# A linear-attention and two-MoE kernel: the scans' constant moves to another PSUM bank, and the small loads, the gate's bias and the padding rows move to other engines and times

## The chip, the cores and the metric

The kernel runs on one core of one Trainium2 chip. The metric is the time of one execution in microseconds, the median of three runs. Five engines work side by side, each on its own queue in order: TensorE (PE), VectorE (DVE), ScalarE (ACT), GpSimd (POOL) and SyncE (SP), which only issues DMAs here.

## The reference

```python
def _attn_ref(q, k, v, alpha):                 # 4 batches, 8 heads, 768 steps, 48 wide
    for t in range(S):
        state = alpha[:, :, t, :, None] * state + einsum('bhd,bhe->bhde', k[:, :, t], v[:, :, t])
        y[:, :, t] = einsum('bhd,bhde->bhe', q[:, :, t], state)
...
def _moe_ref(x, modality_id, w_gate, modality_bias, w1, w2):     # 3072 tokens, 8 experts
    logits = x @ w_gate + modality_bias[modality_id]
    e_idx = np.argmax(logits, axis=1)
...
        out[mask] = gate_w[mask, None] * (np.maximum(x[mask] @ w1[e], 0.0) @ w2[e])
...
def _moe2_ref(x, w_in, w_out):
    r = np.maximum(x @ w_in, 0.0)
    return (r * r) @ w_out
```

## The kernel before

The work has three parts. The attention goes over 24 chunks of 128 steps (4 batches of 6), and the gate of the first MoE goes along with it; then come the first MoE, sorted by expert, and the second MoE. Only the first part is touched. The order on each engine is that in which the program is written.

A chunk's q, k and alpha lie in one tile `qk` of 112 rows: two heads of 48 rows each, with 16 padding rows between them. `load` fetches it in two pieces for chunks 0 to 2 and in one piece from chunk 3 on. `prep(n)` is the DVE's part of a chunk: a scan forward (`acum`), a reciprocal, a scan backward (`rs`), and two products `qt` and `kt`. Between the two scans stands `kv_sd`, which reads what TensorE put into the PSUM tile `kvc`. Each scan has a second operand `amin`, one constant per row, repeated along the row; it lies in a column of `kvc`. The tracking of waits goes by tiles, so a scan that reads `amin` waits for TensorE's last write into `kvc`, and a write into `kvc` waits for the last scan, though they touch other columns.

TensorE's part of a chunk: `qk_mm` (into the two `sp` tiles, which ACT copies out as `pm`), `k_T` (transposes, which ACT copies out as `kT`), `kv_mm` (from `kT` into `kvc`) and `y_mm` (from `pm`, after GpSimd's `mask` has cleared the upper triangle of it). Iteration n of the loop does `qk_mm(n+1)`, `k_T(n+1)`, `kv_mm(n)`, `mask(n+1)`, `prep(n+3)`, `y_mm(n)`. After every fourth chunk `gate_lg` multiplies the outputs by the gate's weights into the PSUM tile `gps`, ACT copies them, and `back` transposes them into another part of `gps`; `gate_b` writes ranks there too. Ahead of the loop TensorE runs 8 matmuls on a constant tile (`warm(WARM)`) and 5 more (`warm(FILL)`) between `k_T(0)` and `qk_mm(1)`.

DMAs have eight counters, DMAHW0 to DMAHW7, which SP's and ACT's DMAs share. The first eight DMAs take them in turn: chunk 0 takes 0 and 1, chunk 1 takes 2 and 3, the first `vv` takes 4, chunk 2 takes 5 and 6, chunk 3 takes 7. A DMA that gets a counter again is issued only when the DMA that had it has landed, and the engine that issues it waits that long, with all that stands behind it in its queue.

`setup_bias` builds the gate's bias from the modality of each token; `setup_gate` builds constants and ends with a DMA that clears `pbuf`.

Of the kernel before, what the change touches and what calls it, by code (L numbers as in the profile page):

```python
# [11 lines left out]
F32 = mybir.dt.float32  # L12
# [3 lines left out]
I32 = mybir.dt.int32  # L16
# [11 lines left out]
C = 128  # L28
# [29 lines left out]
def body(ctx, tc, qka, v, alpha, mod, wg, mbias, w1, w2, w_in, w_out, out):  # L58
# [44 lines left out]

    def load(n):
        b, c = divmod(n, NCH)
        qk = ld.tile([RP, 2 * NP * C + NP * CA], F32, tag="qk", name="qk", bufs=4)
        if n < 3:
            SY.dma_start(qk[:, 2 * NP * C:], qka[b, c, :, 2 * NP * C:])
            SY.dma_start(qk[:, :2 * NP * C], qka[b, c, :, :2 * NP * C])
        else:  # L110
            SY.dma_start(qk, qka[b, c])
        return qk

    loaded, vs = {}, {}
# [9 lines left out]
    make_identity(nc, ident)  # L124
    A.copy(const.tile([128, 1], F32, name="act0"), ident[:, :1])
    kvc = ps_a.tile([RP, 512], F32, name="kvc")
    amin = kvc[:, 2 * NP * D:2 * NP * D + 1]
    V.memset(amin, AMIN)
    amin = amin.to_broadcast([RP, NP * CA])
    sdt = [at1.tile([RP, SDW], F32, name=f"sd{i}") for i in range(3)]  # L130
# [11 lines left out]
    wg_sb = gc.tile([RP, NP, 32], F32, name="wg_sb")  # L142
    G.memset(wg_sb, 0.0)
    for j in range(2):
        SY.dma_start(wg_sb[64 * j:64 * j + D, :, :NE], wg.rearrange("(p j d) e -> j d p e", j=2, d=D)[j])
    mod_sb = gc.tile([128, NTILE, 2], I32, name="mod_sb")
    SY.dma_start(mod_sb, mod.bitcast(I32).rearrange("p (t w) -> p t w", w=2))
    mb_sb = gc.tile([128, 2, NE], F32, name="mb_sb")
    SY.dma_start(mb_sb, mbias.rearrange("(o m) e -> o m e", o=1).to_broadcast([128, 2, NE]))

    ones_b = gc.tile([128, 128], BF16, name="ones_b")
    lt_b = gc.tile([128, 128], BF16, name="lt_b")
    iot = {}
# [28 lines left out]
    def setup_gate():  # L182
        G.memset(ones_b, 1.0)
        G.affine_select(out=lt_b, in_=ones_b, pattern=[[1, 128]], compare_op=ALU.is_gt, fill=0.0, base=0, channel_multiplier=-1)
        iota_f("rev", [128, 128], [[-1, 128]], 127, 0, F16)
        iota_f("tokid", [128, NTILE], [[128, NTILE]], -NT // 2, 1)
        iota_f("hidx", [128, HC], [[1, HC]], 0, 0)
        iota_f("slj", [128, NBIG + 1], [[1, NBIG + 1]], 0, 0)
        iota_f("edesc", [128, NE], [[-1, NE]], NE, 0)
        iota_f("eidx", [128, NE], [[1, NE]], 0, 0)  # L190
        G.memset(ones8, 1.0)
        G.memset(run, 0.0)
        G.memset(oh_all, 0.0)
        SY.dma_start(pbuf.rearrange("(o n) -> o n", n=C), sdt[2][:(NT + PAD) // C, :C].bitcast(I32))

    def setup_bias():
        modf = gc.tile([128, NTILE, 1], F32, name="modf")
        V.tensor_copy(modf, mod_sb[:, :, 0:1])
        modn = gc.tile([128, NTILE, 1], F32, name="modn")
        V.tensor_scalar(modn, modf, -1.0, 1.0, op0=ALU.mult, op1=ALU.add)  # L200
        lb1 = gc.tile([128, NTILE, NE], F32, name="lb1")
        shp = [128, NTILE, NE]
        V.tensor_tensor(lbias, mb_sb[:, 0:1, :].to_broadcast(shp), modn.to_broadcast(shp), op=ALU.mult)
        V.tensor_tensor(lb1, mb_sb[:, 1:2, :].to_broadcast(shp), modf.to_broadcast(shp), op=ALU.mult)
        V.tensor_add(lbias, lbias, lb1)

    def over(t, sh):
        return t.rearrange("p (o e) -> p o e", o=1).to_broadcast(sh)

    gst = {}  # L210

    def gate_lg(g, i0, i1):
        t0 = GROUPS[g][0]
        lt = gps[:, :128]
        for p in range(NP):
            for i in range(i0, i1):
                q = slice(32 * (i - i0), 32 * (i - i0 + 1))
# [327 lines left out]

    def y_mm(n):
        vv, pm, pr = vs.pop(n), pms.pop(n), preps[n]
        y = ps_a.tile([128, 2, 512], F32, tag="y", name="y")
        cross = n % NCH > 0
        v2 = vv.rearrange("s h d -> s (h d)")  # L550
        quads = [(p, j, HEAD[p][j] % 2, p // 2, (64, D)[HEAD[p][j] % 2]) for p in range(NP) for j in range(2)]
# [199 lines left out]
    preps[0] = prep(0)  # L751
    setup_gate()
    qk_mm(0)
    mask(0)
    k_T(0)
    warm(FILL)
    preps[1] = prep(1)
    loaded[4] = load(4)
    preps[2] = prep(2)
    todo = {}  # L760

    def at(n, where, f):
        todo.setdefault((n, where), []).append(f)
# [557 lines left out]
```

## Time and profile before

| | us |
|---|---|
| median of 3 runs (lowest to highest) | 776.43 (776.18 to 777.32) |
| the profiled execution | 774.81 |
| its span, first to last instruction | 773.0 |
| TensorE busy in the span | 745.1 |
| VectorE busy | 478.0 |
| ScalarE busy | 323.8 |
| GpSimd busy | 166.2 |

The attention part fills about the first 122 us of the span. Time is told from the span's start. A matmul in float32 shows as two records in the trace, and engines overlap one instruction's end with the next one's start by about 0.1 us.

### The profile page before, as it was taken

Reading aid. Unit: us, or ns where it says so; the run is one execution under the profiler, and the core shown is the slowest. Engines: PE = TensorE matmul, PEld = TensorE weight load, DVE = VectorE, ACT = ScalarE, POOL = GpSimd, SP = SyncE. Lnnn points to the kernel's source line nnn. Section 1 sums busy time; section 2 is a strip of 40 time slices with the busy share of each in tenths; the row PEclk is TensorE's granted clock in tenths of the full one; section 3 lists DMA queues with packets and bytes.
Section 4 is the critical chain, followed back from the end, with each engine's and each line's share of the span. In section 5 each row is a group of like instructions: output and inputs, shape, how many; then the busy total and the mean of one; then the engine's idle time right before and its main releaser. Section 6 shows DMA issues by size and latency. Waiting matters only on the chain.

```text
span 773.0 us, 13143 instructions
## 1 busy us (share of the span) xinstructions
PE 745.1 (96%) x5148; PEld 654.0 (85%) x5148; DVE 478.0 (62%) x812; ACT 323.8 (42%) x587; POOL 166.2 (21%) x185
## 2 busy tenths in 40 slices
PE   8898989999999999999999999999999999999994
PEld 6777778898788888889889989999899998999984
DVE  7999997877887867878744444544553333343340
ACT  3446467354444443546533323332332342333340
POOL 3332323234645454431100100010020001002001
PEclk9999999999999999999999999999999999999998
DMA  8988765579877886788300220040010000001001
GB/s 216 266 210 237 208 212 164 167 199 221 158 278 221 214 221 157 251 159 230 126 5 1 66 85 0 11 140 1 0 42 2 1 10 31 1 1 42 0 1 45
DMA packets 42814, 88.89 MB, mean 115 GB/s; under 512 B 11181, under 2 KB 26567, under 8 KB 42743
## 3 DMA queue, kind: packets, MB, share of 16 engines
q1 hardware_dynamic: 39543, 78.13, 36.1%
q0 software_dynamic: 3200, 9.83, 4.6%
q8 instruction: 42, 0.69, 0.4%
q14 instruction: 29, 0.24, 0.1%
HBM read 72.19 MB, written 15.76 MB: 114 GB/s over the span
## 4 chain that ended last, share of the span: by engine, by line
PE 76%; DVE 5%; DMA 2%; ACT 1%; issue 1%; POOL 0%; POOLq 0%; DVEq 0%; ACTq 0%
PE acc L660 8%; PE acc L658 8%; PE acc L659 8%; PE h L659 8%; PE h L660 8%; PE h L658 8%; PE hps L659 4%; PE hps L660 4%; PE oo L658 4%; PE oo L659 4%; PE oo L660 4%; PE hps L658 4%; DMA xg<-xs,ids 1%; DVE w2l L569 1%; PE xt L651 1%
## 5 line engine op out<-in xcount | busy, mean ns | idle before, releaser
L1044 DVE TENSOR_TENSOR r<-r 128x512 f32<-128x512 f32 x96 | 68.7, 716 | 143.8 <-ACT r L1043 143.7
L660 PE MATMUL acc<-w2h,hl 128*128 128x384 f32 x372 | 125.7, 338 | 0.3 <-DVE hl L569 0.2
L658 PE MATMUL acc<-w2h,hh 128*128 128x384 f32 x372 | 125.3, 337 | 0.6 <-ACT hh L568 0.6
L659 PE MATMUL acc<-w2l,hh 128*128 128x384 f32 x372 | 124.9, 336 | 0.0
L1043 ACT ACTIVATE r<-h 128x512 f32<-128x512 f32 x96 | 57.4, 598 | 154.4 <-PE h L660 153.0
L660 PE MATMUL h<-xh,w1l 128*128 128x512 f32 x288 | 113.8, 395 | 0.0
L659 PE MATMUL h<-xl,w1h 128*128 128x512 f32 x288 | 113.6, 395 | 0.0
L658 PE MATMUL h<-xh,w1h 128*128 128x512 f32 x288 | 112.1, 389 | 0.0
L569 DVE TENSOR_TENSOR hl<-r,hh 128x512 fp32r<-128x512 f32 x93 | 64.5, 694 | 63.9 <-PE acc L660 36.4
L1067 POOL DMA_INDIRECT out_dram<-ob,pidx x24 | 23.9, 995 | 366.4 <-ACT ob L1065 328.8
L568 ACT CAST hh<-r 128x512 fp32r<-128x512 f32 x93 | 57.7, 620 | 80.6 <-DVE r L1044 80.6
L658 PEld LDWEIGHTS acc<-w2h,hh 128*128 128x128 f32 x372 | 69.9, 188 | 5.1 <-ACT hh L568 1.0
L659 PEld LDWEIGHTS acc<-w2l,hh 128*128 128x128 f32 x372 | 69.8, 188 | 3.8
L660 PEld LDWEIGHTS acc<-w2h,hl 128*128 128x128 f32 x372 | 69.8, 188 | 1.0 <-DVE hl L569 1.0
L658 PE MATMUL oo<-hh,w2h 128*128 128x512 f32 (+1 forms) x192 | 68.7, 358 | 0.0
L658 PE MATMUL hps<-xh,w1h 128*128 128x512 f32 (+1 forms) x192 | 68.1, 355 | 0.0
L659 PE MATMUL hps<-xl,w1h 128*128 128x512 f32 (+1 forms) x192 | 67.4, 351 | 0.7 <-DVE xl L569 0.7
L660 PE MATMUL oo<-hh,w2l 128*128 128x512 f32 (+1 forms) x192 | 67.3, 350 | 0.0
L659 PE MATMUL oo<-hl,w2h 128*128 128x512 f32 (+1 forms) x192 | 67.2, 350 | 0.0
L660 PE MATMUL hps<-xh,w1l 128*128 128x512 f32 (+1 forms) x192 | 67.1, 350 | 0.0
L660 PEld LDWEIGHTS h<-xh,w1l 128*128 128x128 f32 x288 | 54.0, 188 | 11.5
L659 PEld LDWEIGHTS h<-xl,w1h 128*128 128x128 f32 x288 | 54.0, 187 | 9.2
(217 smaller groups left out, 1281.0 us busy)
## 6 DMA issues: line engine op xcount, KB each, us to landing
qk<-qka_dram SPq DMA_DIRECT2D x21, 679.0 KB, 5.7
raw<-w_dram SPq DMA_DIRECT2D x21, 512.0 KB, 8.1
raw<-w_dram SPq DMA_DIRECT2D x28, 384.0 KB, 4.2
cvr<-w_in_dram SPq DMA_DIRECT2D x12, 512.0 KB, 5.9
cvr<-w_out_dram SPq DMA_DIRECT2D x12, 512.0 KB, 11.6
vv<-v_dram SPq DMA_DIRECT2D x24, 192.0 KB, 6.7
xs<-xb SPq DMA_DIRECT2D x24, 192.0 KB, 3.5
alr<-alpha_dram SPq DMA_DIRECT2D x9, 512.0 KB, 3.4
```

The lines of the kernel that those rows point to most:

```text
L568: A.copy(hi, raw)
L569: V.tensor_sub(lo, raw, hi)
L651: PE.transpose(xt[:, hf * 128:(hf + 1) * 128], xgs[i][:, hf, k * 128:(k + 1) * 128], ident)
L658: PE.matmul(o, ah, bh, start=start, stop=False)
L659: PE.matmul(o, ah, bl, start=False, stop=False)
L660: PE.matmul(o, al, bh, start=False, stop=stop)
L1043: A.activation(r, o, AF.Relu)
L1044: V.tensor_mul(r, r, r)
L1067: G.indirect_dma_start(out=out, out_offset=bass.IndirectOffsetOnAxis(ap=pidx[:, n:n + 1], axis=0), in_=ob, in_offset=None)
```

## The change

The constant `amin` moves from `kvc` to the last column of `gps`, and the gate's logits of the groups inside the loop go into free columns of the output tile `y` of the chunk before, not into `gps`. The loads of the gate's weights, of the modalities and of the bias table and the clearing of `pbuf` are issued by ACT. The five instructions of `setup_bias` run on GpSimd, ahead of the loop. `mask(0)` stands behind `prep(1)` and waits for its last DVE instruction. The `qk` tiles are four fixed ones; from chunk 4 on a load writes only the two times 48 rows with data, in two DMAs.

```diff
@@ load
-        qk = ld.tile([RP, 2 * NP * C + NP * CA], F32, tag="qk", name="qk", bufs=4)
+        if n < 4:
+            qks.append(ld.tile([RP, 2 * NP * C + NP * CA], F32, name=f"qk{n}", bufs=1))
+        qk = qks[n % 4]
...
+        elif n == 3:
+            SY.dma_start(qk, qka[b, c])
         else:
-            SY.dma_start(qk, qka[b, c])
+            for j in range(2):
+                SY.dma_start(qk[64 * j:64 * j + D], qka[b, c, 64 * j:64 * j + D])
...
-    amin = kvc[:, 2 * NP * D:2 * NP * D + 1]
+    gps = ps_g.tile([128, 512], F32, name="gps")
+    amin = gps[:RP, 511:512]
...
-        SY.dma_start(wg_sb[64 * j:64 * j + D, :, :NE], wg.rearrange("(p j d) e -> j d p e", j=2, d=D)[j])
+        A.dma_start(wg_sb[64 * j:64 * j + D, :, :NE], wg.rearrange("(p j d) e -> j d p e", j=2, d=D)[j])
...
-    SY.dma_start(mod_sb, mod.bitcast(I32).rearrange("p (t w) -> p t w", w=2))
+    A.dma_start(mod_sb, mod.bitcast(I32).rearrange("p (t w) -> p t w", w=2))
...
-    SY.dma_start(mb_sb, mbias.rearrange("(o m) e -> o m e", o=1).to_broadcast([128, 2, NE]))
+    A.dma_start(mb_sb, mbias.rearrange("(o m) e -> o m e", o=1).to_broadcast([128, 2, NE]))
@@ setup_gate
-        SY.dma_start(pbuf.rearrange("(o n) -> o n", n=C), sdt[2][:(NT + PAD) // C, :C].bitcast(I32))
+        A.dma_start(pbuf.rearrange("(o n) -> o n", n=C), sdt[2][:(NT + PAD) // C, :C].bitcast(I32))
@@ setup_bias (the four others likewise)
-        V.tensor_copy(modf, mod_sb[:, :, 0:1])
+        G.tensor_copy(modf, mod_sb[:, :, 0:1])
@@ gate_lg, y_mm
-        lt = gps[:, :128]
+        lt = gps[:, :128] if n_y[0] is None else n_y[0][:, 0, 2 * C:3 * C]
...
-        y = ps_a.tile([128, 2, 512], F32, tag="y", name="y")
+        y = n_y[0] = ps_a.tile([128, 2, 512], F32, tag="y", name="y")
@@ ahead of the loop
     qk_mm(0)
-    mask(0)
     k_T(0)
     warm(FILL)
     preps[1] = prep(1)
+    mask(0, last_dve())
+    setup_bias()
     loaded[4] = load(4)
...
-    at(2, "mid", setup_bias)
```

ACT's queue at the program's start, before: the casts of the gate's constants (`rev` to `eidx`), then the copies that `qk_mm(0)` and `k_T(0)` wait to be taken out by.

```order
L125 COPY act_121<-ident 128x1 [waits Pool_49]
L160 CAST rev<-rev_i 128x128 [waits Pool_49]
L160 CAST tokid<-tokid_i 128x24 [waits Pool_49]
L160 CAST hidx<-hidx_i 128x22 [waits Pool_49]
L160 CAST slj<-slj_i 128x6 [waits Pool_49]
L160 CAST edesc<-edesc_i 128x8 [waits Pool_49]
L160 CAST eidx<-eidx_i 128x8 [waits Pool_49]
L507 COPY pm<-sp 128x512 [waits PE_49] x2
```

The same place in the changed kernel:

```order
L151 DMA wg_sb<-wg_dram 48x4x8 [waits DMAHW0_49,Pool_49]
L151 DMA wg_sb<-wg_dram 48x4x8 [waits DMAHW1_49]
L153 DMA mod_sb<-mod_dram 128x48 [waits DMAHW2_49]
L155 DMA mb_sb<-mbias_dram 128x16 [waits DMAHW4_49]
L165 CAST rev<-rev_i 128x128 [waits Pool_49]
L165 CAST tokid<-tokid_i 128x24 [waits Pool_49]
L165 CAST hidx<-hidx_i 128x22 [waits Pool_49]
L165 CAST slj<-slj_i 128x6 [waits Pool_49]
L165 CAST edesc<-edesc_i 128x8 [waits Pool_49]
L165 CAST eidx<-eidx_i 128x8 [waits Pool_49]
L199 DMA pbuf<-sd_128 26x128 [waits DMAHW7_49]
L513 COPY pm<-sp 128x512 [waits PE_49] x2
```

Five DMAs with their counters now stand ahead of ACT's first copy of `pm`; the last of them has the counter of chunk 3's load.

SP's queue behind its first eight loads, before: two `vv` loads, the small loads, the clearing of `pbuf`, then the loads of chunks 4 and 5.

```order
L101 DMA vv<-v_dram 128x384 [waits DMAHW0_49]
L101 DMA vv<-v_dram 128x384 [waits DMAHW1_49]
L145 DMA wg_sb<-wg_dram 48x4x8 [waits DMAHW2_49,Pool_49]
L145 DMA wg_sb<-wg_dram 48x4x8 [waits DMAHW3_49]
L147 DMA mod_sb<-mod_dram 128x48 [waits DMAHW4_49]
L149 DMA mb_sb<-mbias_dram 128x16 [waits DMAHW5_49]
L194 DMA pbuf<-sd_127 26x128 [waits DMAHW6_49]
L111 DMA qk<-qka_dram 112x1552 [waits DMAHW7_49,DVE_49]
L111 DMA qk<-qka_dram 112x1552 [waits DMAHW0_49,DVE_49]
```

The same place in the changed kernel (`qk_99` is the tile of chunks 0, 4, 8 and so on, `qk_102` that of chunks 1, 5, 9):

```order
L101 DMA vv<-v_dram 128x384 [waits DMAHW3_49]
L101 DMA vv<-v_dram 128x384 [waits DMAHW5_49]
L116 DMA qk_99<-qka_dram 48x1552 [waits DMAHW1_49,DMAHW6_49,DMAHW0_49,DVE_49]
L116 DMA qk_99<-qka_dram 48x1552 [waits DMAHW0_49]
L116 DMA qk_102<-qka_dram 48x1552 [waits DMAHW2_49,DMAHW1_49,DVE_49]
L116 DMA qk_102<-qka_dram 48x1552 [waits DMAHW2_49]
```

The small loads are gone from there, each load of a chunk is two DMAs, and the load of chunk 4 waits for the counters 0, 1 and 6, no longer for 7.

DVE's queue from the product `kt` of chunk 5 to the forward scan of chunk 6, before (`SCALAR_TENSOR_TENSOR` is a scan here):

```order
L483 TENSOR_TENSOR kt<-qk,rs 112x512 [waits DVE_49]
L198 CAST modf<-mod_sb 128x24 [waits DMAHW4_49]
L200 TENSOR_SCALAR modn<-modf 128x24 [waits DVE_49]
L203 TENSOR_TENSOR lbias<-mb_sb,modn 128x192 [waits DMAHW5_49,DVE_49]
L204 TENSOR_TENSOR lb_433<-mb_sb,modf 128x192
L205 TENSOR_TENSOR lbias<-lbias,lb_433 128x192 [waits DVE_49]
L472 SCALAR_TENSOR_TENSOR acum<-qk,kvc 112x528 [waits DMAHW2_49,PE_49]
```

And in the changed kernel, up to the first read of `kvc` in chunk 6:

```order
L489 TENSOR_TENSOR kt<-qk_102,rs 112x512 [waits DVE_49]
L478 SCALAR_TENSOR_TENSOR acum<-qk_107,gps 112x528 [waits DMAHW5_49,DMAHW4_49]
L479 RECIPROCAL qk_107<-acum 112x4 [waits DVE_49]
L549 TENSOR_TENSOR sd_126<-kvc,sd_128 112x192 [waits PE_49,Pool_49]
L483 SCALAR_TENSOR_TENSOR rs<-qk_107,gps 112x528 [waits DVE_49]
```

The five instructions of the bias have left DVE, and the forward scan has no wait for TensorE there; that wait now stands at the instruction that reads `kvc`. Of the 24 forward scans 18 waited for a matmul into `kvc` before; 7 wait for one into `gps` now: those of chunks 7, 11, 15 and 19 for `back`, 12 and 20 for `gate_b`, and 23 for the matmuls of the first slot's ids, which stand behind `back`.

## Rows read from the trace of the kernel before

**Rows 1.** The page, part 1: busy us (share of span) and instructions of each engine.

```profile
PE 745.1 (96%) x5148; PEld 654.0 (85%) x5148; DVE 478.0 (62%) x812; ACT 323.8 (42%) x587; POOL 166.2 (21%) x185
```

**Rows 2.** Busy time by stretch: us, each engine's busy us, clock, DMA share, GB/s.

```profile
100.00:120.00 20.00, 18.79 (x332) 15.57 (x332) 17.42 (x42) 12.99 (x30) 8.10 (x13) 1.00 0.67 225
```

**Rows 3.** The chain that ended last, 60 to 126 us: start, us, what.

```profile
105.90 0.60 PE xtr L293 x4
```

**Rows 4.** Waits, 0 to 130 us: who waited for whom, us in total, times, longest.

```profile
PE kvc L529 <- DVE rs L477: 4.9, 7, 1.1
DVE acum L472 <- DMA qk<-qka_dram: 3.6, 2, 2.7
DVE acum L472 <- PE kvc L529: 2.4, 4, 1.1
```

**Rows 5.** Timeline of DVE: start, us, line, instruction, [idle before <- what ended it].

```profile
10.23 1.07 DVE L481 TENSOR_TENSOR qt<-qk,acum 112x512 f32<-112x512 f32 x1
...
14.92 0.67 DVE L481 TENSOR_TENSOR qt<-qk,acum 112x512 f32<-112x512 f32 x1
...
16.11 1.25 DVE L472 TENSOR_TENSOR_SCAN acum<-qk,kvc 112x528 f32<-112x528 f32 x1
...
17.48 0.33 DVE L541 TENSOR_TENSOR sd<-kvc,acum 112x192 f32<-112x192 f32 x1
...
21.00 1.25 DVE L472 TENSOR_TENSOR_SCAN acum<-qk,kvc 112x528 f32<-112x528 f32 x1 [0.84 <-DMA qk<-qka_dram]
...
28.95 0.17 DVE L198 CAST modf<-mod_sb 128x24 f32<-128x24 int32 x1
...
30.30 1.24 DVE L472 TENSOR_TENSOR_SCAN acum<-qk,kvc 112x528 f32<-112x528 f32 x1
...
50.43 1.25 DVE L472 TENSOR_TENSOR_SCAN acum<-qk,kvc 112x528 f32<-112x528 f32 x1 [0.33 <-PE kvc L529]
...
80.22 1.25 DVE L472 TENSOR_TENSOR_SCAN acum<-qk,kvc 112x528 f32<-112x528 f32 x1 [0.58 <-PE kvc L529]
```

**Rows 6.** Timeline of TensorE, the first two chunks, and two places later.

```profile
9.80 2.34 PE L136 MATMUL warm<-wrm 112*128 112x256 f32 x10
12.48 1.16 PE L504 MATMUL sp<-qt,kt 48*128 48x128 f32 x16 [0.34 <-DVE kt L483]
...
15.06 0.61 PE L529 MATMUL kvc<-vv,kT 128*64 128x48 f32 x15 [0.88 <-DVE rs L477]
...
50.31 0.33 PE L226 MATMUL gps<-ident,ls 128*128 128x128 f32 x1
...
97.72 0.61 PE L293 MATMUL xtr<-ident,yt 112*128 112x112 f32 x4 [1.62 <-ACT xb L297]
```

**Rows 7.** Timeline of ACT: the first copies of `pm`.

```profile
9.46 1.07 ACT L507 COPY pm<-sp 128x512 f32<-128x512 f32 x2 [5.49 <-PE sp L504]
```

**Rows 8.** Timeline of SP's DMA issues: start, us the issuing took, line.

```profile
12.77 0.41 SPq L194 DMA_DIRECT2D pbuf<-sd  x1
15.68 1.73 SPq L111 DMA_DIRECT2D qk<-qka_dram  x2
```

**Rows 9.** DMA packets in the stretch 14 to 16 us.

```profile
DMA packets 877, 0.29 MB, mean 144 GB/s; under 512 B 711, under 2 KB 874, under 8 KB 877
```

**Rows 10.** Timeline of GpSimd: its product of 192 columns.

```profile
22.79 0.52 POOL L544 TENSOR_TENSOR sd<-sd,acum 112x192 f32<-112x192 f32 x1 [1.29 <-DVE sd L543]
```

**Rows 11.** Busy time by stretch at the span's end; the clock stands behind GpSimd's column.

```profile
763.00:763.50 0.50, 0.25 (x2) 0.00 (x0) 0.00 (x0) 0.21 (x1) 0.00 (x0) 1.00 0.04 15
...
765.00:765.50 0.50, 0.00 (x0) 0.00 (x0) 0.00 (x0) 0.00 (x0) 0.50 (x1) 0.91 0.00 0
765.50:766.00 0.50, 0.00 (x0) 0.00 (x0) 0.00 (x0) 0.00 (x0) 0.23 (x1) 0.50 0.00 0
```

**Rows 12.** The tile `warm`: ns shortest/median/longest, starts; 1 to 5 us, then 9 to 13.

```profile
L136 PE MATMUL warm<-wrm x8: 634/634/796, 1.7 to 4.8; 112*128 112x256 f32 x8
...
L136 PE MATMUL warm<-wrm x10: 379/379/395, 9.8 to 11.8; 112*128 112x256 f32 x10
```

More of the change, by code (lines that the diff above doesn't have):

```diff
@@ L109, in load @@
             SY.dma_start(qk[:, :2 * NP * C], qka[b, c, :, :2 * NP * C])
-        else:
-            SY.dma_start(qk, qka[b, c])
+        elif n == 3:
+            SY.dma_start(qk, qka[b, c])
+        else:
+            for j in range(2):
+                SY.dma_start(qk[64 * j:64 * j + D], qka[b, c, 64 * j:64 * j + D])
         return qk
-    loaded, vs = {}, {}
+    loaded, vs, qks = {}, {}, []
     for n in range(2):
@@ L153, in body @@
     iot = {}
-    gps = ps_g.tile([128, 512], F32, name="gps")
     def iota_f(name, shape, pattern, base, cm, dt=F32):
@@ L193, in setup_gate @@
         G.memset(oh_all, 0.0)
-        SY.dma_start(pbuf.rearrange("(o n) -> o n", n=C), sdt[2][:(NT + PAD) // C, :C].bitcast(I32))
+        A.dma_start(pbuf.rearrange("(o n) -> o n", n=C), sdt[2][:(NT + PAD) // C, :C].bitcast(I32))
     def setup_bias():
         modf = gc.tile([128, NTILE, 1], F32, name="modf")
-        V.tensor_copy(modf, mod_sb[:, :, 0:1])
+        G.tensor_copy(modf, mod_sb[:, :, 0:1])
         modn = gc.tile([128, NTILE, 1], F32, name="modn")
-        V.tensor_scalar(modn, modf, -1.0, 1.0, op0=ALU.mult, op1=ALU.add)
+        G.tensor_scalar(modn, modf, -1.0, 1.0, op0=ALU.mult, op1=ALU.add)
         lb1 = gc.tile([128, NTILE, NE], F32, name="lb1")
         shp = [128, NTILE, NE]
-        V.tensor_tensor(lbias, mb_sb[:, 0:1, :].to_broadcast(shp), modn.to_broadcast(shp), op=ALU.mult)
-        V.tensor_tensor(lb1, mb_sb[:, 1:2, :].to_broadcast(shp), modf.to_broadcast(shp), op=ALU.mult)
-        V.tensor_add(lbias, lbias, lb1)
+        G.tensor_tensor(lbias, mb_sb[:, 0:1, :].to_broadcast(shp), modn.to_broadcast(shp), op=ALU.mult)
+        G.tensor_tensor(lb1, mb_sb[:, 1:2, :].to_broadcast(shp), modf.to_broadcast(shp), op=ALU.mult)
+        G.tensor_add(lbias, lbias, lb1)
     def over(t, sh):
@@ L210, in body @@
     gst = {}
+    n_y = [None]
     def gate_lg(g, i0, i1):
         t0 = GROUPS[g][0]
-        lt = gps[:, :128]
+        lt = gps[:, :128] if n_y[0] is None else n_y[0][:, 0, 2 * C:3 * C]
         for p in range(NP):
@@ L849, in body @@
     actx.close()
+    n_y[0] = None
     ps_y = pool(gctx, "ps_y", space=PSUM, side="right")
```

## The prediction

> **What bounds the kernel now.** I read the page first. TensorE is busy 96% of the span [rows 1], so what follows the attention is a row of matmuls, and a microsecond won or lost ahead of it is won or lost at the end. The change touches only the attention, the first 122 us. There the view by stretches shows two engines near full side by side, TensorE with 18.8 of 20 us and DVE with 17.4 [rows 2], and nothing throttled. The chain that ended last runs through that part from 105.9 us on, and it is TensorE's queue [rows 3]; before that, records are missing and the chain can't be followed, so I lay out the two queues myself from the timeline.
>
> The waits say how the two hold each other. TensorE's `kv_mm` waited 4.9 us in 7 places for a backward scan; DVE's forward scans waited 2.4 us in 4 places for `kv_mm`, and 3.6 us in 2 places for a load [rows 4], of which 0.84 us lies at chunk 4 [rows 5] and the rest is the first load, which nothing here changes.
>
> **The change, part by part.** The profiled execution took 774.81 us, 1.8 more than its span; the median is 776.43. I work out a difference and put it on the median.
>
> *The bias.* It takes DVE from 28.95 to 30.30 us, where the next scan follows at once [rows 5]: 1.35 us off a full queue. On GpSimd it is three products of 192 columns and two small instructions; a product of that width took 0.52 us there [rows 10], so about 2 us, behind `mask(0)` and ahead of `mask(1)`. GpSimd sits idle in that stretch, and `y_mm(1)`, which needs `mask(1)`, comes late anyway (below). Were the products twice as slow, `mask(1)` and what follows would be up to 1 us later. I count no cost, and 1 us for the upper end.
>
> *The loads.* A load of 96 rows for 112 saves a seventh of the bytes. DVE waited for no load but the two named, so the bytes are worth nothing by themselves. What counts is chunk 4: its load was issued at 15.68 us, because the clearing of `pbuf` stood ahead of it until 12.77 and then it waited for counter 7 [rows 8]. Now it waits for counters 0, 1 and 6, and counter 6 is the one for which `pbuf` waited until 12.77. It goes out nearly 3 us earlier, and the 0.84 us at 21.00 go. That the load is two DMAs is one more issue of some 0.4 us on SP, which has time.
>
> *`mask(0)`.* It ran beside `qt` of chunk 1, which took 1.07 us there and 0.67 in chunk 2 [rows 5]. Moving it gives DVE 0.4 us and perhaps as much on the product behind it. But chunk 3's load lands only at about 15.7 (below) and the scan that needs it began at 16.11, so at most 0.4 of that can be used, and the next step hides all of it.
>
> *The small loads on ACT.* This is the cost. ACT's queue now holds five DMAs ahead of its first copy of `pm`, and the last waits for counter 7, which is chunk 3's load. When does that land? SP's issue at 15.68 was waiting for the same counter; its other wait, `prep(0)`, had long been met. So ACT is held until 15.68, spends 0.41 us on the issue as SP did [rows 8], and makes the two copies in 1.07 us [rows 7]: they end at 17.16, where they ended at 10.53. `qk_mm(1)` needs both `sp` tiles back; it began at 12.48 and begins at 17.16 now. From its start to the end of `kv_mm(0)` lay 15.67 - 12.48 = 3.19 us, of which 0.88 was a wait for a scan [rows 6] that the change removes: 2.31 us of work, so 19.47. DVE's read of `kvc` stood at 17.48 [rows 5] and now waits for that: 2.0 us later.
>
> *TensorE's clock.* `warm(FILL)` ends at 12.14 [rows 6], so TensorE now stands idle for 5.0 us. At the span's end its last matmul is over at about 763.25, and in the stretch from 765.0 the granted clock falls from full to half, 2.2 us later [rows 11]. An idle time of 1.62 us in the middle [rows 6] left it full. [...] Then the 2.31 us become up to 4.62: `kv_mm(0)` ends at 21.78, and DVE is 4.3 us late. If the clock stays up, 2.0 late; with the ratio 634 to 379 in place of two, 3.5.
>
> *The scans' constant.* It takes away false waits, but some come back. Seven forward scans now wait for a matmul into `gps`, among them three of the four that waited in the profile. At 50.43 the scan waited for `kvc`; now it would wait for the transposition behind it, from 50.31 to 50.64 [rows 5, 6]. The same stands at chunks 15 and 23. Only the 0.58 us at 80.22 [rows 5] are surely gone. TensorE's 4.9 us are waits in a queue that was early; they let it catch up, which it needs now, but where the gate's choices come from DVE it still follows DVE. I count 0.3, between 0 and the 2.4 of all four.
>
> *The sum.* Late by 4.3, less 0.84, 1.35 and 0.3: 1.8 us slower, 778.2 us. TensorE begins 4.7 us late and loses 2.3 more at the low clock; the waits of rows 4 give back most of that by mid-stage, so it isn't later than DVE for long.
>
> [...] The clearing and the small loads put 711 packets under 512 B through in 2 us, at 144 GB/s [rows 9] where the stage has 225 [rows 2]: (225 - 144) x 2 = 160 KB less, or 0.7 us of transfer. They went last before; now four of them go in among the big loads. [...] No row of before has the two queues at once, so I leave it out of the sum and keep it as a rival.
>
> **The rivals.**
>
> *The clock stays up,* or is back before `qk_mm(1)` is through. For it: the granted clock is full all through the attention. Against it: 5.0 us of idle against the 2.2 that were enough at the end. Then 2.0 - 0.84 - 1.35 - 0.3 = -0.5: 775.9 us, no change that can be told.
>
> *ACT is not held,* and the kernel is faster. This would be so if chunk 3's load landed early, or the copies did not stand behind the DMA. The point is 12.48 - 1.07 = 11.4 us: a hold that ends by then delays nothing, and each microsecond beyond it costs about one. Then 0.84 + 1.35 + 0.3 = 2.5 us are won: 773.9. Against it: SP was held by these counters until 12.77 and 15.68 in this very program [rows 8], and the order puts the copy behind the wait.
>
> *The loads interleave,* as above, and the low clock lasts on. 0.7 us for the later landing, and TensorE at half level for 1.5 us more, which loses 0.75 of its work: 778.2 + 1.5 = 779.7.
>
> **How the numbers follow.** A difference under 0.2%, 1.55 us, is about what a measurement of this kernel can't tell from none; slower begins at 777.98, faster ends at 774.88. The case of the sum, 50%: from 777.3 (the ratio of durations) to 779, slower in about 32 of the 50. Clock stays up, 25%: nearly all of it the same. ACT not held, 12%: faster. Interleaved loads, 13%: slower. Together faster 0.14, same 0.41, slower 0.45. The likeliest time is 778.2. The range takes in the clock's rival with half a microsecond below it, and the interleaved loads: 775.4 to 780.0; outside lie ACT not held and the far ends. The sum's own case alone is 777.3 to 779.3.
>
> **What will show it.** ACT's first copy of `pm` at about 16.1 us instead of 9.46, with ACT's wait in front of it ended by a DMA; `qk_mm(1)` at about 17 us; matmuls there that take nearly twice their time, or a granted clock of half; DVE's first read of `kvc` idle before it by 2 to 4 us, ended by `kv_mm`; no bias on DVE; chunk 4's scan not waiting for its load; scans of chunks 11, 15 and 23 waiting, if at all, for matmuls into `gps`. From the second group of chunks on the two traces should run at one pace, a fixed distance apart. I am wrong if ACT copies `pm` before 12 us, or if the distance at 50 us isn't that at 120.

## The result: slower by 4.1 us, and the profile after

The changed kernel takes 780.55 us (median of 6, 779.21 to 783.63), the kernel before in the same comparison 776.49 (6 runs, 775.02 to 777.32): 1.0057 times as long, 95% interval 1.0036 to 1.0077. The prediction said 778.2 us and at most 780.0; the direction was right and the loss twice as large. The profiled execution after is the longest of its six, so I took a second trace of the same kernel ("again", below) and read both. A ratio leaves disturbed executions out, here and below, and need not be the quotient of the medians.

Two stretches of the first trace differ most from before. The first is the one predicted. This is ScalarE's timeline: "ACTq" is the issue of a DMA, and the bracket is the idle time before an instruction and what ended it.

```profile
14.95 0.60 ACTq L199 DMA_DIRECT2D pbuf<-sd  x1
15.59 1.07 ACT L513 COPY pm<-sp 128x512 f32<-128x512 f32 x2 [5.00 <-DMA qk<-qka_dram]
```

The first copy of `pm` stands at 15.59 us, 9.46 before [rows 7], and a chunk load ended its wait, as the prediction had it. What TensorE makes of it is in its timeline, where a second place stands out:

```profile
16.23 2.56 PE L510 MATMUL sp<-qt,kt 48*128 48x128 f32 x16 [4.62 <-ACT pm L513]
...
34.59 1.06 PE L224 MATMUL y<-yt,wg_sb 112*32 112x128 f32 x27
37.67 0.41 PE L224 MATMUL y<-yt,wg_sb 112*32 112x128 f32 x5 [2.02 <-issue]
38.02 0.67 PE L535 MATMUL kvc<-vv,kT 128*64 128x48 f32 x16
38.61 0.33 PE L232 MATMUL gps<-ident,ls 128*128 128x128 f32 x1
```

The sixteen records of `qk_mm(1)` take 2.56 us, 1.16 before [rows 6]: 2.2 times as long. In the middle of the first group's logits, between the 27th and the 28th of 32 records, TensorE then stands still for 2.02 us, and the trace has "issue" there, which means that no semaphore held it. The view by stretches gives the clock (the figure behind GpSimd's column):

```profile
16.00:18.00 2.00, 1.77 (x14) 1.77 (x15) 0.74 (x2) 1.10 (x3) 1.59 (x4) 0.50 1.08 197
...
20.00:22.00 2.00, 2.00 (x29) 2.00 (x27) 1.13 (x2) 0.30 (x1) 0.85 (x2) 0.50 1.03 190
22.00:24.00 2.00, 2.00 (x25) 1.44 (x21) 2.00 (x4) 0.99 (x2) 0.00 (x0) 0.92 1.06 197
...
36.00:38.00 2.00, 0.33 (x5) 0.14 (x4) 0.00 (x0) 0.00 (x0) 0.91 (x2) 1.00 1.07 220
38.00:40.00 2.00, 2.00 (x35) 1.79 (x33) 1.02 (x1) 0.27 (x1) 0.00 (x0) 0.85 1.02 205
...
42.00:44.00 2.00, 2.00 (x18) 1.78 (x16) 2.00 (x3) 0.56 (x2) 0.00 (x0) 0.50 0.05 17
...
46.00:48.00 2.00, 2.00 (x37) 1.49 (x34) 2.00 (x3) 0.59 (x1) 0.00 (x0) 0.94 1.02 169
```

TensorE's granted clock is 0.50, half of the full one, from 16 to 22 us and, after the stop at 36 us, from 39 to 46 us once more. Before, it reads 1.00 in every stretch from 0 to 122 us. VectorE shows what both cost:

```profile
20.87 0.36 DVE L547 TENSOR_TENSOR sd<-kvc,acum 112x192 f32<-112x192 f32 x1 [4.09 <-POOL pm L499]
...
23.49 1.25 DVE L478 TENSOR_TENSOR_SCAN acum<-qk,gps 112x528 f32<-112x528 f32 x1
...
31.48 1.25 DVE L478 TENSOR_TENSOR_SCAN acum<-qk,gps 112x528 f32<-112x528 f32 x1
...
38.98 1.25 DVE L478 TENSOR_TENSOR_SCAN acum<-qk,gps 112x528 f32<-112x528 f32 x1 [3.44 <-PE gps L232]
...
57.22 1.25 DVE L478 TENSOR_TENSOR_SCAN acum<-qk,gps 112x528 f32<-112x528 f32 x1 [1.40 <-PE gps L232]
...
86.67 1.25 DVE L478 TENSOR_TENSOR_SCAN acum<-qk,gps 112x528 f32<-112x528 f32 x1
...
119.62 1.25 DVE L478 TENSOR_TENSOR_SCAN acum<-qk,gps 112x528 f32<-112x528 f32 x1 [1.72 <-PE gps L339]
```

The first row is the read of `kvc`, 17.48 before. The trace names GpSimd's mask as what released it. It follows the end of `kv_mm(0)` by 0.1 us here and in the second trace, and in warm_through, below, it stands ahead of that mask's end, so I take `kv_mm(0)` for the releaser. Against the scans of before [rows 5], chunk 4's is 2.5 us late (23.49 for 21.00, and no longer waits for its load), chunk 6's 1.2 (31.48 for 30.30, the bias being gone from VectorE), chunk 11's 6.8 (57.22 for 50.43), chunk 17's 6.5 (86.67 for 80.22). The jump lies between, at chunk 7: its scan waits 3.44 us for the transposition into `gps`, which stands behind the logits. Of the 8.9 us by which this span is longer 7.7 are there by the last scan (119.62 for 111.93); what came later I did not follow.

### The profile page after: what moved, and what is told of

Same layout as the page of the kernel before. It is cut to its first block, busy times and chain, and to the rows that moved or that the text cites. A ratio compares the mean times of both kernels' runs of the same rounds, so it can differ in the third digit from the quotient of the medians.

```text
span 781.9 us, 13162 instructions
## 1 busy us (share of the span) xinstructions
PE 750.1 (96%) x5148; PEld 658.2 (84%) x5148; DVE 475.9 (61%) x807; ACT 323.5 (41%) x587; POOL 168.9 (22%) x190
## 4 chain that ended last, share of the span: by engine, by line
PE 73%; DVE 6%; DMA 3%; ACT 2%; issue 1%; SPq 0%; POOL 0%; POOLq 0%; DVEq 0%; ACTq 0%
PE acc L666 8%; PE acc L664 8%; PE acc L665 8%; PE h L665 8%; PE h L666 8%; PE h L664 8%; PE hps L666 4%; PE oo L664 4%; PE oo L665 4%; PE hps L665 4%; PE oo L666 4%; PE hps L664 4%; DMA raw<-w_dram 2%; DVE w2l L575 1%; PE xt L657 1%
## 5 line engine op out<-in xcount | busy, mean ns | idle before, releaser
L665 PE MATMUL hps<-xl,w1h 128*128 128x512 f32 (+1 forms) x192 | 67.4, 351 | 0.6 <-DVE xl L575 0.6
## 6 DMA issues: line engine op xcount, KB each, us to landing
qk<-qka_dram SPq DMA_DIRECT2D x40, 291.0 KB, 5.7
```

What stands on the lines that cost most here:

```text
L665: PE.matmul(o, ah, bl, start=False, stop=False)
```

## The experiments

I had three theories at first, HOLD (that of the prediction), BANK and LOADS, which the first expectation spells out, and after four runs a fourth, FETCH. Fifteen runs follow. Each was timed against the kernel before on the same chip, and "ratio" is its time over that of before with a 95% interval. "Clock" is the median over the executions of the mean granted clock, "over 778.5" how many of the executions were longer than that.

| run | median us | before us | ratio (interval) | clock | over 778.5 |
|---|---|---|---|---|---|
| again (changed kernel) | 780.90 | 776.62 | 1.0056 (1.0035 to 1.0077) | 0.9885 | 5 of 6 |
| pbuf_sp | 783.19 | 776.62 | 1.0064 (1.0033 to 1.0095) | 0.9880 | 9 of 12 |
| amin_kvc | 779.60 | 776.62 | 1.0053 (1.0029 to 1.0077) | 0.9890 | 9 of 12 |
| loads_old | 779.45 | 776.62 | 1.0040 (1.0028 to 1.0053) | 0.9890 | 10 of 12 |
| only_halves | 779.52 | 777.67 | 1.0023 (0.9999 to 1.0048) | 0.9910 | 8 of 12 |
| only_small_act | 778.91 | 777.67 | 1.0030 (1.0009 to 1.0051) | 0.9910 | 9 of 12 |
| only_bank | 777.43 | 777.67 | 1.0000 (0.9980 to 1.0021) | 0.9930 | 3 of 12 |
| only_bias_pool | 776.12 | 777.67 | 0.9990 (0.9966 to 1.0014) | 0.9925 | 5 of 12 |
| warm_through | 779.45 | 776.31 | 1.0039 (1.0009 to 1.0070) | 0.9905 | 6 of 12 |
| old_loads_pbuf_sp | 778.45 | 776.31 | 1.0015 (0.9987 to 1.0043) | 0.9925 | 6 of 12 |
| bank_bias | 778.75 | 776.31 | 1.0021 (0.9998 to 1.0044) | 0.9900 | 8 of 12 |
| only_columns | 775.61 | 776.31 | 0.9986 (0.9966 to 1.0007) | 0.9945 | 0 of 12 |
| warm_cols | 776.30 | 777.16 | 0.9979 (0.9957 to 1.0002) | 0.9935 | 2 of 12 |
| cols_bias | 776.99 | 777.16 | 0.9996 (0.9973 to 1.0018) | 0.9925 | 3 of 12 |
| cols_fill | 774.25 | 777.16 | 0.9969 (0.9950 to 0.9988) | 0.9955 | 0 of 12 |

The executions of one kernel differ by 3 to 14 us, and in most kernels the long ones are those with the low clock; in thirteen of the fifteen runs time and clock correlate at -0.63 to -0.99, and loads_old and cols_fill, whose executions keep within about 3 us, show no such tie. The ratios count before the medians.

**again.** No edit.

> The changed kernel as it is, for a second trace. Theories. HOLD: the ACT queue stands behind the store of the padding rows until 15.6 us, TensorE idles 4.6 us, runs at half clock from 16 to 22 us, and all later delays follow from that lag. BANK: the scans that share a bank with the gate's transposes wait for TensorE in the gate's groups (3.44, 1.40, 0.63, 0.50 and 1.72 us in the first trace), and this is a cost of its own. LOADS: the split loads move fewer bytes per microsecond (182 against 256 GB/s in 30 to 45 us) and later transfers pay. All three expect 779.5 to 781.5 us here. HOLD and BANK expect the wait of the scan before the first gate group's transpose again, at 3 us or more. If the 2.02 us in which TensorE stood still in the middle of the first group's logits at 35.6 us is chance, it is absent or elsewhere here.

The stop comes at the same record, shorter:

```profile
33.85 1.06 PE L224 MATMUL y<-yt,wg_sb 112*32 112x128 f32 x27
35.83 0.41 PE L224 MATMUL y<-yt,wg_sb 112*32 112x128 f32 x5 [0.92 <-issue]
```

TensorE keeps its clock behind it, and the scan of chunk 7 waits 2.44 us. Chunk 6's scan is 0.3 us late in this trace and chunk 11's 2.5. The stop stands at one place in both traces; its length varies.

**pbuf_sp.** Undoes one line of the change:

```diff
-        A.dma_start(pbuf.rearrange(...
+        SY.dma_start(pbuf.rearrange(...
```

> The changed kernel with the store of the padding rows back on SP's queue, at the same place of the program; nothing else undone. HOLD expects ScalarE's first copy of pm before 11 us, no TensorE idle of over 2 us before 20 us, full clock, and a time of 776 to 777.5 us, 3 to 4.5 us under the changed kernel; the scans' waits for the gate's transposes shrink with the lag. BANK expects 779 to 780.5 us: the waits for the gate's bank stay. LOADS expects 780 to 781 us.

HOLD as the whole reason fails here: without the hold the kernel is no faster, and its executions spread from 774.43 to 788.53 us. The trace is of the longest of them, so I take the reason from old_loads_pbuf_sp. It has the stop at the same record too, and two later ones of 3.20 and 1.48 us:

```profile
36.65 0.42 PE L224 MATMUL y<-yt,wg_sb 112*32 112x128 f32 x5 [2.19 <-issue]
```

**amin_kvc.** The scans' operand back in `kvc` and the logits in `gps`:

```diff
-    amin = gps[:RP, 511:512]
+    amin = kvc[:, 2 * NP * D:2 * NP * D + 1]
-        lt = gps[:, :128] if n_y[0] is None else n_y[0][:, 0, 2 * C:3 * C]
+        lt = gps[:, :128]
```

> The changed kernel with the scans' operand back in the bank of the kv outputs and the gate's logits back in the gate's bank; nothing else undone. HOLD expects 779.5 to 781.5 us, as the changed kernel: TensorE still starts late, and the scans wait for kv matmuls in place of the gate's. BANK expects 777 to 778.5 us: the five scans' waits (7.7 us in sum, of which the lag explains about half) go. LOADS expects 780 to 781 us.

The ratio is that of the changed kernel, where BANK expected 2 to 3 us less. BANK finds no support here, though the two intervals alone leave it room; only_bank, below, bounds it.

**loads_old.** Chunk loads as before, in one transfer of 112 rows.

> The changed kernel with the chunk loads as before: four buffers of one pool, 112 rows in one transfer from chunk 3 on; nothing else undone. LOADS expects 245 GB/s or more in 20 to 40 us and 777 to 778.5 us. HOLD and BANK expect the rate to rise and the time to stay, 779.5 to 781.5 us, since in the first trace one scan alone waits for a load.

The rate in 16 to 50 us is 226 GB/s, TensorE doesn't stop in the logits, and the ratio falls from 1.0056 to 1.0040, which the intervals don't tell apart; the time lies at the edge of what HOLD expected. The executions keep within 3 us of one another. From the stops and rates of these traces came FETCH: slow loads make loads and instructions late.

**only_halves.** The first of four kernels that add one part of the change to the kernel before: the loads.

> The kernel before with one part of the change: four tiles of chunks by name, and from chunk 4 on two transfers of 48 rows in place of one of 112. FETCH (new theory): the 48-row transfers keep the DMA engines as busy for fewer bytes (190 GB/s against 250 in 16 to 50 us of the runs so far), so loads, and the instruction blocks that TensorE's sequencer fetches through the same engines, land late by an amount that differs between executions; it expects a median of 777 to 780 us, a spread between executions of over 4 us, and a wait of TensorE for nothing but instructions of about 1 us or more before 60 us. HOLD and BANK, if they alone explain the loss, expect 775.5 to 777 us here with the spread of before (some 3 us).

Slower by about 1.8 us by the ratio's middle, with an interval that just reaches none. The executions spread by 8.4 us, but those of the kernel before spread by 7.5 on this chip, so the spread says nothing for FETCH. Its trace has TensorE's stop, and then VectorE's wait:

```profile
30.05 1.06 PE L223 MATMUL gps<-yt,wg_sb 112*32 112x128 f32 x27
34.48 0.65 PE L223 MATMUL gps<-yt,wg_sb 112*32 112x128 f32 x5 [3.37 <-issue]
```

```profile
36.20 1.25 DVE L477 TENSOR_TENSOR_SCAN acum<-qk,kvc 112x528 f32<-112x528 f32 x1 [3.05 <-PE kvc L534]
```

Here the scan waits for `kvc` as in the kernel before: whichever bank holds the operand, the scan waits for the matmuls behind the logits. TensorE's clock is half from 33 to 40 us. What comes ahead of the stop's end shows in the DMA view: in the quarter of a microsecond from 31.50 a packet of an instruction queue begins, and takes 33.8% of 16 engines' 0.25 us, or 1.35 us of one engine.

```profile
q8 instruction: 1, 0.02, 33.8%
```

TensorE goes on at 34.48, 3.0 us later. In the other traces with this stop the same packet begins 2.8 to 3.2 us ahead of the 28th record (34.50 for 37.67, 32.75 for 35.83, 33.75 for 36.65 in pbuf_sp, 30.25 for 33.30 in only_bias_pool, 29.75 for 32.52 in bank_bias). In the kernel before it began at 29.25, and TensorE lost 0.3 us in the same logits, which take 1.42 us there and 1.08 in the later groups:

```profile
31.07 1.42 PE L218 MATMUL gps<-yt,wg_sb 112*32 112x128 f32 x32
```

So the time from packet to record is nearly the same in all six stops, and what differs is how early the packet begins against TensorE: 1.8 us ahead of the logits in the kernel before, 1.5 behind their start in only_halves. That the packet holds TensorE's next instructions is inferred from these distances, and from the counts: in the kernel before this queue has 42 packets for TensorE's 10,296 records (matmuls and weight loads), and 4 of them in each 100 us from 200 to 700 us, where TensorE's records go from 901 to 1,059 and the other engines' from 116 to 227. Of the six traces with 48-row loads (the two of the changed kernel, pbuf_sp, amin_kvc, only_halves, warm_through) each has a stop of 0.9 us or more before 130 us, four of them at this record; of eleven with 112 rows two have, both with the bias on GpSimd.

**only_small_act.** The small loads and the clearing of `pbuf` on ScalarE's queue, alone.

> The kernel before with one part of the change: the gate's small loads and the store of the padding rows on ScalarE's queue. HOLD expects ScalarE's first copy of pm at 15 us or later, TensorE idle 3 us or more ahead of chunk 1's matmuls and at half clock behind it, and a time of 778.5 to 780 us: the 2.8 us that are left of the loss when the loads are as before. FETCH and BANK expect 776 to 777.5 us.

As HOLD expected in mechanism: ScalarE's first copy stands at 14.52 us (15 or later was expected), TensorE idles 3.55 us, and the ratio makes 2.3 us. VectorE's timeline, the forward scans of chunks 3, 4 and 6:

```profile
18.82 1.25 DVE L472 TENSOR_TENSOR_SCAN acum<-qk,kvc 112x528 f32<-112x528 f32 x1 [3.43 <-PE kvc L529]
...
22.79 1.25 DVE L472 TENSOR_TENSOR_SCAN acum<-qk,kvc 112x528 f32<-112x528 f32 x1
...
32.09 1.25 DVE L472 TENSOR_TENSOR_SCAN acum<-qk,kvc 112x528 f32<-112x528 f32 x1
```

Chunk 3's scan waits 3.43 us for `kv_mm(0)`. Against [rows 5] chunk 4's is 1.8 us late (22.79 for 21.00), chunk 6's 1.8 (32.09 for 30.30) and chunk 17's, at 82.02, the same 1.8: one loss at the start, carried on.

**only_bank.** The operand in `gps` and the logits beside the outputs, alone.

> The kernel before with one part of the change: the scans' operand in the gate's bank and the gate's logits beside the outputs. BANK expects 777.5 to 779 us: the scans at 34, 50, 70, 86 and 112 us wait for the gate's transposes, each later than the kv matmuls that they waited for before. HOLD and FETCH expect 775.5 to 776.8 us: without a late TensorE these waits are small, and the waits for kv matmuls (2.4 us in 4 rows) go.

No difference, to 0.2% either way. Its trace shows another source of the spread:

```profile
97.49 1.01 PE L294 MATMUL xtr<-ident,yt 112*128 112x112 f32 x4 [1.62 <-ACT xb L298]
```

```profile
96.00:98.00 2.00, 0.51 (x3) 0.51 (x4) 1.79 (x12) 1.30 (x4) 0.00 (x0) 0.78 0.00 0
98.00:100.00 2.00, 2.00 (x23) 1.72 (x21) 2.00 (x7) 1.67 (x4) 0.00 (x0) 0.50 0.78 226
```

```profile
115.13 1.25 DVE L473 TENSOR_TENSOR_SCAN acum<-qk,gps 112x528 f32<-112x528 f32 x1 [4.54 <-PE gps L334]
```

The 1.62 us wait for ScalarE near 97 us stands in the kernel before too [rows 6], and left the clock full there. Here it falls to half for about 7 us, and the last scan waits 4.54 us for matmuls into `gps`. Thirteen of the seventeen traces have this wait, at 1.62 or 1.63 us: in six the clock stays full, in seven it is at half during the wait or within 1.5 us of its end.

**only_bias_pool.** The bias on GpSimd and `mask(0)` later, alone.

> The kernel before with one part of the change: the five bias operations on GpSimd, and chunk 0's mask behind chunk 1's scans. All theories expect VectorE without the five rows at 28 us (1.3 us); if the start of the attention stage is what the end follows, 774.9 to 776 us, and if GpSimd's two microseconds between the masks of chunks 0 and 1 hold up TensorE's second output, 776 to 777.5 us.

Seven executions at 772.5 to 776.4 us, five at 779.1 to 781.0; the ratio tells nothing from no change. Chunk 6's scan stands at 27.79 us for 30.30, but TensorE, now at the logits at 29.91, waits 2.32 us in the middle of them with no semaphore: a gain that one wait takes back.

**warm_through.** More warm-up under the hold:

```diff
-    warm(FILL)
+    warm(FILL + 7)
```

> The changed kernel with 7 more warm-up matmuls behind chunk 0 (12 in place of 5, 24 rows in place of 10; they compute nothing that is used), which carry TensorE to about 15.3 us, close to the end of ScalarE's hold. CLOCK (the lag at the start is in good part the half clock at 16 to 22 us): the granted clock stays at 1.00 from 14 to 22 us, chunk 1's sixteen sp rows take 1.2 us and not 2.56, VectorE reads kvc at 18 to 19 us and not at 20 to 21, and the median falls by 1 to 2.5 us to 778 to 779.5 us. If the idle time alone sets the lag, the time stays within 0.5 us of the changed kernel's 780.5 to 780.9 us.

The clock stays at 1.00 and the start is what the prediction's first rival said. The stretch from 16 us, then TensorE's and VectorE's timelines:

```profile
16.00:18.00 2.00, 1.96 (x20) 1.65 (x20) 0.56 (x2) 1.40 (x4) 1.77 (x5) 1.00 1.02 201
```

```profile
16.04 1.64 PE L510 MATMUL sp<-qt,kt 48*128 48x128 f32 x16 [1.58 <-ACT pm L513]
```

```profile
18.93 0.36 DVE L547 TENSOR_TENSOR sd<-kvc,acum 112x192 f32<-112x192 f32 x1 [2.34 <-PE kvc L535]
...
29.71 1.25 DVE L478 TENSOR_TENSOR_SCAN acum<-qk,gps 112x528 f32<-112x528 f32 x1
```

VectorE reads `kvc` at 18.93, not 20.87, and chunk 6's scan is 0.6 us ahead of before (29.71 for 30.30); chunk 11's, 50.13 for 50.43, 0.3 ahead. The median gains little, because later stops remain: in this trace 3.04 us without a semaphore at 95 to 98 us, and half clock from 98 to 104.

**old_loads_pbuf_sp.** loads_old and pbuf_sp together.

> The changed kernel with two parts undone: the chunk loads as before and the store of the padding rows on SP's queue. Left are the bank, the bias on GpSimd and the gate's three small loads on ScalarE's queue. If the parts add up (halves +1.8, hold +2.3, bank 0, bias -0.8 us in the runs of one part alone), 775 to 776.8 us on a chip where before takes 776.5. If the small loads on ScalarE's queue cost by themselves (in the run with the store on SP, mod_sb landed at 17.4 us and the mask of chunk 1 waited 4.2 us behind the bias), 777 to 778.5 us, with TensorE waiting for a mask near 20 us.

By its median and its trace the second of the two, but the interval reaches both. GpSimd's timeline, then TensorE's:

```profile
15.99 0.20 POOL L198 CAST modf<-mod_sb 128x24 f32<-128x24 int32 x1 [3.26 <-DMA mod_sb<-mod_dram]
...
18.18 3.30 POOL L494 TENSOR_SCALAR_AFFINE_SELECT pm<-pm 128x512 f32<-128x512 f32 x4
```

```profile
19.33 0.66 PE L555 MATMUL y<-pm,vv 128*48 128x128 f32 x2 [1.61 <-POOL pm L494]
```

The bias waits 3.26 us for `mod_sb`, and the masks of chunks 1 and 2 stand behind the bias on GpSimd. `y_mm(1)` waits 1.61 us, and the clock is half from 19 to 29 us. With the hold this was covered, since TensorE was late anyway; the hold gone, it shows. ScalarE's queue is only part of it. In only_bias_pool, where SP issues that load, the bias waits for it too, and it lands 0.7 us earlier:

```profile
15.30 0.28 POOL L198 CAST modf<-mod_sb 128x24 f32<-128x24 int32 x1 [2.28 <-DMA mod_sb<-mod_dram]
```

In bank_bias, also with SP's queue, `modf` stands at 15.43 and `y_mm(1)` waits 0.31 us. Of the 1.3 us more that it waits here, 0.56 are the later load, 0.44 a first mask that takes 1.07 us and not 0.63, and 0.29 TensorE's earlier arrival.

**bank_bias.** Two parts on the kernel before.

> The kernel before with two parts of the change: the scans' operand in the gate's bank with the logits beside the outputs, and the bias on GpSimd with chunk 0's mask behind chunk 1's scans. Additive parts expect 0.5 to 1 us less than before, 775.3 to 776.2 us on a chip where before takes 776.5; BANK as a cost of its own expects more than before. The last scan's wait for the gate's bank is expected at 0.5 us where TensorE keeps its full clock through 95 to 105 us and at 3 us or more where it does not.

More than before by the ratio's middle, but the interval reaches none; the trace has the stop of 2.24 us at the logits and half clock in 34 to 37 and 98 to 102 us. The gain did not come; that the bank is at fault isn't shown.

**only_columns.** The kernel before with two transfers per chunk again, but of all rows:

```diff
-                SY.dma_start(qk[64 * j:64 * j + D], qka[b, c, 64 * j:64 * j + D])
+                SY.dma_start(qk[:, h * j:h * j + h], qka[b, c, :, h * j:h * j + h])
```

> The kernel before with its chunk loads from chunk 4 on in two transfers of all 112 rows and half of the columns each, in the four tiles by name: as many transfers as with the 48-row halves and the bytes of before. If the 48 rows (a part of the partitions to land in) make the DMA engines slow, the rate in 20 to 40 us is 240 GB/s or more and the time 776 to 777.5 us, as before. If the number of transfers does it, the rate is near 200 GB/s and the time 778 us or more.

The rows do it, not the number of transfers, and not the four fixed tiles, which this kernel has too. The DMA view from 16 to 50 us, only_halves, then only_columns: all packets, the loads' queue (packets, MB, share of 16 engines), and one load's KB and median us from issue to landing:

```profile
DMA packets 2243, 6.66 MB, mean 196 GB/s; under 512 B 407, under 2 KB 1430, under 8 KB 2237
...
q1 hardware_dynamic: 2237, 6.58, 95.0%
...
qk<-qka_dram SPq DMA_DIRECT2D x16, 291.0 KB, 7.8
```

```profile
DMA packets 3787, 8.59 MB, mean 253 GB/s; under 512 B 464, under 2 KB 1616, under 8 KB 3780
...
q1 hardware_dynamic: 3780, 8.49, 90.3%
...
qk<-qka_dram SPq DMA_DIRECT2D x18, 339.5 KB, 4.2
```

34 us of 16 engines are 544 engine-us. The halves use 95.0% of it for 6.58 MB, 78.5 engine-us per MB; the columns 90.3% for 8.49 MB, 57.9. A chunk of two times 291.0 KB in halves then costs 45.7 engine-us, one of two times 339.5 KB in columns 39.3. The kernel before, in one transfer, used 63.1 per MB in that stretch and 42.9 a chunk:

```profile
q1 hardware_dynamic: 2488, 8.54, 99.1%
```

The measure is rough (in three traces the share passes 100%), but it parts the halves from the rest: 78.5 to 86.0 engine-us per MB in the six traces with halves, 60.4 to 67.4 in the seven with one transfer, 57.9 to 66.2 in the four with columns. For a chunk that makes 45.7 to 50.1, 41.0 to 45.8 and 39.3 to 45.0; columns and one transfer aren't told apart. Per MB the halves in only_halves take 1.36 times the engine time of the columns in only_columns. Why isn't shown: no run parts the number of rows in a transfer, 48 or 112, from the place where they land.

**warm_cols.** The changed kernel with more warm-up and column loads.

> The changed kernel with 7 more warm-up matmuls, as in warm_through, and with chunk loads from chunk 4 on in two transfers of all 112 rows and half of the columns. If the half clock behind the hold and the 48-row transfers are the whole loss, 775.3 to 776.8 us on a chip where before takes 776.3, with the scans of chunks 7 to 10 some 0.5 us earlier than in the first trace of before. If the bank or the small loads on ScalarE's queue cost something by themselves, 777.5 us or more.

The loss is gone: ratio 0.9979 (0.9957 to 1.0002), against 1.0056 of the changed kernel. Chunk 11's scan is 0.5 us ahead of before [rows 5]:

```profile
49.96 1.25 DVE L479 TENSOR_TENSOR_SCAN acum<-qk,gps 112x528 f32<-112x528 f32 x1
```

Against warm_through only the form of the loads differs, and the ratio falls from 1.0039 to 0.9979: some 4.7 us, and the two intervals don't meet. That is the strongest evidence against the halves.

**cols_bias.** Column loads and the bias on GpSimd.

> The kernel before with column halves in named tiles, the bias on GpSimd and chunk 0's mask behind chunk 1's scans; bank and queues as before. If the bias's 1.35 us on VectorE reach the end, 774 to 775.2 us where before takes 776.3. If TensorE, now earlier at the first group's logits, waits there for its instructions (2.2 to 2.3 us in the two runs with the bias on GpSimd and loads as before) and loses its clock, 776 to 778 us.

No stop at the logits, and its shortest execution, 771.3 us, is the shortest of all; but in the trace the clock falls near 95 us, and the ratio is 0.9996. The bias's gain stands in the trace until then (chunk 11's scan at 47.97 us, 49.50 in only_columns) and is gone at the last scan (112.26 for 111.00); the median shows none.

**cols_fill.** Column loads, and matmuls that nothing reads in the wait near 97 us:

```diff
+    def fill(k):
+        kp = ps_a.tile([128, NP, RP], F32, tag="kp", name="kp")
+        for i in range(k):
+            PE.matmul(kp[:, :2, :], wrm[:, :128], wrm[:, :2 * RP], start=True, stop=True)
+
+    at(18, "A", lambda: fill(4))
```

> The kernel before with column halves in named tiles, and 4 matmuls of 224 columns (nothing reads them) ahead of the transposes that wait 1.62 us for ScalarE near 97.5 us. If TensorE's clock, when it falls in that wait, is what makes some executions 3 to 5 us longer, none of the executions has a granted clock under 0.992 or a time over 778.5 us, and the median falls to 774.5 to 775.5 us. If not, the times spread as without them (773.3 to 776.9 us for the columns alone, 773.6 to 780.4 us for before).

```profile
95.16 1.78 PE L793 MATMUL kp<-wrm 112*128 112x224 f32 x8
96.86 0.60 PE L299 MATMUL xtr<-ident,yt 112*128 112x112 f32 x4
```

The transposes follow without a wait. All twelve executions lie between 773.50 and 776.55 us with a clock of 0.994 or more, and the ratio is 0.9969 (0.9950 to 0.9988): faster than both kernels, by 0.3% against the kernel before. What the filling adds to the columns isn't shown. The columns alone have 0.9986 (0.9966 to 1.0007), a spread of 3.6 us and no execution over 778.5 either, and no run fills the wait without the columns.

## Why the prediction was wrong

The step that failed is "The loads". It says that a load of 96 rows for 112 saves a seventh of the bytes, worth nothing by itself, and prices the split as one more issue. What the split does to the DMA engines has no term in the sum. The runs put there 45.7 to 50.1 engine-us a chunk against 41.0 to 45.8 in one transfer, for a seventh fewer bytes, and a ratio of 1.0023 (0.9999 to 1.0048) for the halves alone against 0.9986 (0.9966 to 1.0007) for the columns: about 1.8 us against the kernel before, 2.9 against the columns, and 4.7 between warm_through and warm_cols, where the rest of the change is in place. The prediction looked for waits for a load, and in the traces of the changed kernel and of only_halves no scan but the first has one. What these traces have is TensorE's stops without a semaphore and, in two of the three, the half clock behind them. The profile of before had the warning: from 16 to 50 us the loads' queue already took 99.1% of the DMA engines, so a change of how rows land had to be priced there. It isn't the second transfer by itself that costs: in those 34 us the two row halves moved 196 GB/s and the two column halves 253.

Point by point:

- *The small loads on ACT* was right in mechanism and near in size. Predicted: ACT's copy at about 16.1, `qk_mm(1)` at 17.16, `kvc` read 2.0 to 4.3 us late. Measured: 15.59, 16.23 and 3.4 us late (20.87 for 17.48), in the second trace 14.75, 15.39 and 2.6. `qk_mm(1)` did not need both `sp` tiles back: it began behind the first copy. From its start to the read of `kvc` lay 4.64 us in both traces, where the sum at half clock had 4.62. So this term was too large by 0.9 to 1.7 us, and the miss lies elsewhere. Alone the part costs 1.8 us at every later chunk and 2.3 by the ratio.
- *TensorE's clock* was right: half from 16 to 22 us. warm_through confirms the price of the other case, chunk 6's scan 0.6 us ahead of before where -0.5 was predicted; with half clock it is 1.2 late, or 0.3 in the second trace, where +1.8 was predicted. The sum thus had the start 0.6 to 1.5 us too late. How long the low clock lasts after such an idle time no row of before shows, and the sum has TensorE at half of its rate for 4.6 us; after the hold it worked at 0.50 from 16.2 to 22.3 us. That the first matmuls' 634 ns for 379 [rows 12], the ratio behind the low end, come from the clock isn't shown either: it reads 1.00 from 0 to 12 us. But I asked for the clock only there. The idle times that took it again at 36 us, and in other executions near 97 us, are where the traces show the rest of the loss. (The sum's low end, by the ratio of durations, comes to 777.4 and not 777.3.)
- *The bias* at no cost held only under the hold's cover. Its 1.35 us did leave VectorE; on GpSimd it took 2.2 us (17.43 to 19.67), about as predicted. Without the hold it waits for `mod_sb` and holds up the masks, a wait that has no term in the prediction.
- *The scans' constant* is worth nothing in either direction (ratio 1.0000, to 0.2%). Waits moved from `kvc` to `gps`, which stand a fraction of a microsecond apart in TensorE's queue.
- "*From the second group of chunks on at one pace*" fails: the distance is 1.2 us at chunk 6, 6.8 at chunk 11 and 7.7 at the last scan; in the second trace 0.3, 2.5 and 3.4.
- The rival that the loads interleave came nearest in time (779.7), by luck. Its 0.7 us for a later landing no run shows: the load that releases ACT landed earlier than I had it, not later (ACT's issue stands at 14.95 us, where I had 15.68). Its second half, that the low clock lasts on, holds: TensorE worked at half clock for some 6 us (16.2 to 22.3) where the sum had 4.6. But the start was no later for it, and the loss came later on.

What adds up: the ratios of the four parts alone, +0.30% (hold), +0.23% (halves), 0 (bank) and -0.10% (bias), make +0.43%, against +0.57% measured, with intervals of some 0.2% on each. In us that is +2.3, +1.8, 0 and -0.8, where the sum had +3.5 (the hold less chunk 4's load), 0, -0.3 and -1.35. That the parts simply add isn't shown: taking the halves out of the changed kernel took off 0.16% (loads_old), out of warm_through 0.60%. What stays open is what sets the moment at which the packet of the instruction queue begins (only_halves, above); that slow loads delay it fits the counts above, but two kernels with 112-row loads had the stop as well, and the kernel before, with its engines as full (99.1%), had none. Nor is it settled why the same 1.62 us wait costs the clock in seven traces and not in six.

## What to carry to other kernels

Price a DMA by the engine time it takes, not by its bytes: here a chunk in two sets of 48 rows, 582 KB, took 45.7 engine-us, and one of 112 rows in one transfer, 679 KB, 42.9. A DMA queued on an engine that also computes can hold all that stands behind it, as ScalarE's first copy of `pm`, at 15.59 us for 9.46, so look which transfer it waits for before moving it there. Where a kernel's executions spread by several microseconds, look for idle times of TensorE with the low clock behind them (in only_halves a stop of 3.37 us, and half clock from 33 to 40 us). Work that nothing needs kept the clock at the start here (1.00 in warm_through from 16 to 18 us, 0.50 in the changed kernel); near 97 us the filled kernel was the fastest, but what the filling did there isn't parted from the loads.

## What the runs showed of the hardware

TensorE stopped for 0.9 to 3.4 us in the middle of a row of matmuls with no semaphore to wait for, at the same record in six traces, some 3 us after a packet of an instruction queue began on the DMA engines. The same wait of 1.62 us left the granted clock full in six traces and was followed by the half clock in seven. And 112 rows in two column halves moved at 253 GB/s where two sets of 48 rows moved at 196, in the same 34 us of otherwise equal kernels.
